# A large weight-gradient store sent as a row scatter, with eight of its 128 rows sent apart

## The chip, the cores and the metric

The kernel runs on one core of one Trainium2 chip. The metric is device time in microseconds (us) of one execution. The six runs of the kernel before lie within 0.2% of each other (730.99 to 732.42 us), so differences of a few tenths of a per cent are read only from several runs on the same chip beside the kernel before.

## The reference

The reference computes one decode step and all its gradients: a layer norm, a 32-head attention over a cache of 8192 positions, and beside it a gated MLP, whose outputs are added.

```python
def _fwd_reference(A_x, A_k_cache, A_v_cache, A_wq, A_wo, B_x, B_w1, B_w3, B_w2):
    # cut: _A_ref is attention with one query row per head; _B_ref is silu(x@w1) * (x@w3) @ w2
    xn = _layernorm(A_x, axis=-1)
    return A_x + _A_ref(xn, A_k_cache, A_v_cache, A_wq, A_wo) + _B_ref(xn, B_w1, B_w3, B_w2)

def reference(...):                      # outputs: out and the gradients of 8 inputs
    _out, _vjp = jax.vjp(_f, A_x, A_k_cache, A_v_cache, A_wq, A_wo, B_w1, B_w3, B_w2)
    ...
```

The caches are (1, 32, 8192, 128) in bf16, so K and V are 67 MB each. They are read once and their gradients are written once. That is 268 MB of the 303.5 MB that the kernel moves. The gradient of w2 is (1728, 640), 2.2 MB.

## The kernel before

One head's K or V is one tile of 128 partitions by 16,384 B (2 MB). It is loaded, used, overwritten by its gradient and stored. Ten such slots rotate. SP (SyncE) issues all these loads and stores in program order.

```python
    def fifo(out_, in_):
        nc.sync.dma_start(out_, in_)
    # cut
    def load_next():
        # cut: next head in turn, next free slot
        fifo(t[:], (kc if kind == "K" else vc)[h])
    # cut
    def store(kind, h):
        t = kv_tiles.pop((kind, h))
        # cut
        fifo((dkc if kind == "K" else dvc)[h], t[:])
        free_slots.append(t)
        load_next()
```

The MLP runs once, early, between the second and the third head. Its weights borrow four of the ten slots. Slot `mD` holds 12 of the 14 row blocks of w2, with 12 rows of 1280 B, or 15,360 B, per partition. Their gradient is written into the same tile and stored from GpSimd. The slot then goes back to the rotation, and SP issues the next load.

```python
    w2a = mD[:, 0:NBA * D].rearrange("p (b c) -> p b c", c=D)
    # cut
        for b in range(NBA):
            nc.vector.tensor_scalar(w2a[:, b, :], g_bc[:], hcol[:, b:b + 1], None, ALU.mult)
        nc.gpsimd.dma_start(out_8[0:NBA * P, :].rearrange("(p fb) c -> p fb c", fb=NBA), w2a)
        # cut: the small rest of w2, from GpSimd too
        free_slots.append(mD)
        load_next()
```

## Time and profile before

| what | before |
|---|---|
| time, median of 3 runs | 732.32 us (731.69 to 732.42) |
| time beside the changed kernel, median of 6 runs | 731.98 us (730.99 to 732.42) |
| span of the profiled run | 729.3 us |
| DMA engines | 90% or more busy in 39 of 40 slices, mean 416 GB/s |
| the stretch 718 to 728 us | no compute; DMA share 0.38, then 0.06 |

The lines themselves stand in the prediction. The page is read for the bound (busy shares, then the digit rows), and the table of windows for the end. There the DMA share is the mean busy share of the 16 engines.

One more view is used below, and this is how to read it. In the trace of the kernel before, the four semaphores that SP alone uses show 1136 steps for 71 transfers, 16 for each. I take them as one step per engine, of which the page counts 16. The time from the first to the last step is called its **lag** here. Read so, it tells how far the slowest of the 16 engines is behind the fastest. I read the steps from the trace's semaphore records; the steps carry no engine names.

### The profile page before, as it was taken

What the parts mean: (1) busy time and instruction counts of PE and PEld (TensorE: products, weight loads), DVE (VectorE), ACT (ScalarE), POOL (GpSimd) and SP (SyncE); (2) the same over time, 40 slices, a digit from 0 to 9 for tenths busy, and PEclk for the clock granted to TensorE, in tenths of its full rate; (3) what the DMA queues carried; (4) which work ended last, traced back from release to release, by engine and by line L of the source; (5) the groups of instructions that cost most, each with busy time, mean ns of one, the idle gap of its engine ahead of it and who ended that gap; (6) DMA issues with size and microseconds to landing.
All of it is one profiled execution on the core that took longest, in us unless ns stands there. A gap on an engine that the chain in (4) does not pass through costs nothing.

```text
span 729.3 us, 12910 instructions
## 1 busy us (share of the span) xinstructions
PE 603.3 (83%) x5193; PEld 376.2 (52%) x5193; DVE 461.1 (63%) x811; ACT 376.1 (52%) x727; POOL 29.9 (4%) x45
## 2 busy tenths in 40 slices
PE   3989589999999999987987987887898879977930
PEld 2546356665566556644554554454465545645510
DVE  4068655677767776767556764655746775667581
ACT  3640736665666656644554554554564545555510
POOL 0010110000100000001000000000000000000000
PEclk9995799999999999999998999998989999999965
DMA  9999999999999999999999999999999999999994
GB/s 344 398 409 422 427 428 425 400 426 422 416 415 428 429 426 424 428 430 426 424 429 429 430 425 427 425 430 429 423 430 425 429 430 429 428 429 429 429 413 183
DMA packets 27135, 303.53 MB, mean 416 GB/s; under 512 B 2798, under 2 KB 4146, under 8 KB 10434
## 3 DMA queue, kind: packets, MB, share of 16 engines
q1 hardware_dynamic: 21328, 276.39, 89.8%
q0 software_dynamic: 5728, 26.30, 8.9%
q8 instruction: 41, 0.67, 0.4%
q14 instruction: 20, 0.16, 0.1%
q10 hardware_dynamic: 18, 0.01, 0.0%
HBM read 151.34 MB, written 151.34 MB: 415 GB/s over the span
## 4 chain that ended last, share of the span: by engine, by line
DMA 48%; PE 38%; DVE 6%; ACT 4%; issue 1%; SPq 0%; ACTq 0%; DVEq 0%
DMA out_dram<-kv 21%; DMA kv<-in_A_k_cache_dram 18%; PE pT L318 18%; DMA kv<-in_A_v_cache_dram 7%; PE sA L339 5%; PE X L433 4%; PE dA L339 4%; DVE kv L466 3%; PE m L356 2%; DMA wo_g<-in_A_wo_dram 2%; ACT KT L320 1%; ACT kv L630 1%; PE gu_ps L549 1%; PE dh_ps L560 1%; PE acc L199 1%
## 5 line engine op out<-in xcount | busy, mean ns | idle before, releaser
L320 ACT COPY KT<-pT 128x512 f32<-128x512 f32 x512 | 288.2, 588 | 228.1 <-PE pT L318 208.6
L318 PE MATMUL pT<-ident_f,kv 128*128 128x128 f32 x2048 | 306.6, 289 | 58.5 <-DMA kv<-in_A_k_cache_dram 32.7
L318 PEld LDWEIGHTS pT<-ident_f,kv 128*128 128x128 f32 x2048 | 235.8, 148 | 151.1 <-PE pT L318 49.7
L466 DVE TENSOR_TENSOR kv<-qd,U 128x4096 bf16<-128x4096 bf16 x64 | 146.0, 2284 | 0.0
L466 DVE TENSOR_TENSOR kv<-qd,P 128x4096 bf16<-128x4096 bf16 x64 | 143.6, 2285 | 0.0
L433 PE MATMUL X<-kv,Z 128*32 128x512 bf16 x1024 | 96.9, 413 | 1.8 <-DVE Z L450 1.8
L339 PE MATMUL dA<-KT,qz 128*32 128x512 bf16 x512 | 83.5, 405 | 0.0
L339 PE MATMUL sA<-KT,qz 128*32 128x512 bf16 x512 | 83.0, 404 | 0.0
L416 DVE SCALAR_TENSOR_TENSOR U<-m,P 128x64 bf16<-128x64 f32 x32 | 7.5, 233 | 85.1 <-PE m L356 85.1
L433 PEld LDWEIGHTS <-Z 128*32 128x32 bf16 x1024 | 33.0, 100 | 35.2 <-issue 8.3
L339 PEld LDWEIGHTS <-qz 128*32 128x32 bf16 x1024 | 29.5, 95 | 40.7 <-issue 38.1
L382 DVE TENSOR_REDUCE mrow<-m 128x1 f32<-128x64 f32 x32 | 7.1, 223 | 68.3 <-PE m L356 68.3
L356 PE MATMUL m<-selc,KT 64*128 64x64 f32 x256 | 30.7, 243 | 8.1 <-ACT KT L346 8.1
L356 PEld LDWEIGHTS m<-selc,KT 64*128 64x128 f32 x256 | 21.7, 145 | 30.2 <-ACT KT L346 20.2
L376 ACT CAST qd<-pT 128x256 bf16<-128x256 f32 x32 | 11.9, 372 | 40.5 <-DVE kv L466 31.5
L389 DVE TENSOR_REDUCE negM<-m 128x1 f32<-128x128 f32 x32 | 9.3, 292 | 33.3 <-PE m L386 33.3
L514 DVE SCALAR_TENSOR_TENSOR wq_g<-wq_g,side 128x512 bf16<-128x512 bf16 x40 | 27.3, 682 | 0.0
L257 DVE SCALAR_TENSOR_TENSOR side<-wo_g,g_bc 128x640 bf16<-128x640 bf16 x32 | 26.2, 820 | 1.0 <-DMA wo_g<-in_A_wo_dram 0.7
L448 DVE SCALAR_TENSOR_TENSOR U<-m,P 128x128 bf16<-128x128 f32 x32 | 11.4, 355 | 16.8 <-PE m L446 16.8
L406 DVE RECIPROCAL rZ<-m 128x1 f32<-128x1 f32 x32 | 5.3, 167 | 24.2 <-PE m L400 24.2
L346 ACT COPY KT<-dA 64x512 f32<-64x512 f32 x32 | 18.6, 582 | 2.7 <-PE dA L339 2.7
L346 ACT COPY KT<-sA 64x512 f32<-64x512 f32 x32 | 18.6, 581 | 1.1 <-PE sA L339 0.8
(161 smaller groups left out, 374.8 us busy)
## 6 DMA issues: line engine op xcount, KB each, us to landing
out_dram<-kv SPq DMA_DIRECT2D x64, 2048.0 KB, 31.0
kv<-in_A_k_cache_dram SPq DMA_DIRECT2D x32, 2048.0 KB, 26.3
kv<-in_A_v_cache_dram SPq DMA_DIRECT2D x32, 2048.0 KB, 26.3
out_dram<-wo_g POOLq DMA_DIRECT2D x8, 640.0 KB, 11.8
out_dram<-wq_g POOLq DMA_DIRECT2D x8, 640.0 KB, 13.2
wq_g<-in_A_wq_dram POOLq DMA_DIRECT2D x7, 640.0 KB, 13.5
wo_g<-in_A_wo_dram POOLq DMA_DIRECT2D x7, 640.0 KB, 19.3
kv<-in_B_w_dram SPq DMA_DIRECT2D x2, 1728.0 KB, 29.3
```

Of the source, the lines that this page charges most:

```text
L257: nc.vector.scalar_tensor_tensor(junk[:], G_["wo"][:, hh, :], 1.0, g_bc[:], ALU.mult, ALU.mult, accum_out=G_["do"][:, hh:hh + 1])
L318: nc.tensor.transpose(pT[:, k * P:(k + 1) * P], W3[:, 4 * c + k, :], ident_f[:])
L320: nc.scalar.copy(KT[:].rearrange("p k w -> p (k w)"), pT[:])
L339: nc.tensor.matmul(S_[kind][q:q + QW, :], lhsT=S_["qz"][:, o:o + QW], rhs=KTb[c][:, par, :], start=(c0 == 0 and par == 0), stop=(c0 == NCH ...
L346: nc.scalar.copy(XS[0:QH].rearrange("p k w -> p (k w)"), S_.pop(kind)[0:QH, :])
L356: nc.tensor.matmul(S_["m"][:, b0:b0 + 4 * J].rearrange("p (x c k t) -> p k x c t", x=4, k=4, t=2)[:, k], lhsT=XS[0:QH, k, :], rhs=selc[0:Q ...
L376: nc.scalar.copy(qd[:].rearrange("p a d -> p (a d)"), hd[h].pop("ps_r"))
L389: nc.vector.tensor_reduce(S_["negM"][:], S_["m"][:, 2 * J:2 * J + P], AX.X, ALU.max, negate=True)
L433: nc.tensor.matmul(xg["X"][q:q + QW, :], lhsT=Z[:, o:o + QW], rhs=W[:, N4 * i:N4 * (i + 1)], start=(slot == 0 and i < 4), stop=(slot == NS ...
L448: nc.vector.scalar_tensor_tensor(S_["U2"][:], S_["V"][:, 0:J].unsqueeze(2).to_broadcast([P, J, 2]), S_["m"][:, OC + NS:OC + NS + 1], S_["P ...
L466: nc.vector.tensor_tensor(dst[:, lo * DH:hi * DH].rearrange("p (j a b) -> p j a b", a=DH // 2, b=2), vec.rearrange("p (a b) -> p a b", b=2 ...
L514: nc.vector.scalar_tensor_tensor(wq_g[:, ci, :], wq_g[:, ci, :], 1.0, dqb, ALU.mult, ALU.mult, accum_out=dxa[:, ci, g:g + 1])
```

## The change

The intent: one engine ends last, so take from it the eight rows of the w2 gradient store that it would carry, and give these rows to engines that end earlier. The store becomes a scatter with a list of row numbers. In the list, the partitions 16-19 and 48-51 get a number past the end (their own plus 256), and such rows are dropped. The dropped rows leave from SP as two transfers of four rows.

```diff
-    masks = consts.tile([P, 4], F32, name="masks")
+    masks = consts.tile([P, 8], F32, name="masks")
@@
+    R0 = 16
+    sidx = masks[:, 4:5].bitcast(mybir.dt.int32)
+    nc.gpsimd.iota(sidx, pattern=[[0, 1]], base=0, channel_multiplier=1)
+    skip = masks[:, 5:6]
+    nc.vector.tensor_reduce(skip, ident_f[:, 0:2 * QW].rearrange("p (a w) -> p a w", w=QW)[:, :, R0:R0 + 4],
+                            AX.XY, ALU.add)
+    nc.vector.scalar_tensor_tensor(sidx, skip, float(2 * P), sidx, ALU.mult, ALU.add)
+
+    def scatter_store(dst, t):
+        nc.gpsimd.indirect_dma_start(out=dst, out_offset=bass.IndirectOffsetOnAxis(ap=sidx, axis=0),
+                                     in_=t, in_offset=None, bounds_check=P - 1, oob_is_err=False)
+        for r0 in (R0, R0 + QW):
+            fifo(dst[r0:r0 + 4], t[r0:r0 + 4])
@@
-        nc.gpsimd.dma_start(out_8[0:NBA * P, :].rearrange("(p fb) c -> p fb c", fb=NBA), w2a)
+        scatter_store(out_8[0:NBA * P, :].rearrange("(p fb) c -> p (fb c)", fb=NBA), mD[:, 0:NBA * D])
```

## The prediction

> **What bounds the kernel now.** I read the page first: busy shares, the slices, the DMA queues, the chain.
>
> ```profile
> span 729.3 us, 12910 instructions
> ...
> PE 603.3 (83%) x5193; PEld 376.2 (52%) x5193; DVE 461.1 (63%) x811; ACT 376.1 (52%) x727; POOL 29.9 (4%) x45
> ...
> DMA  9999999999999999999999999999999999999994
> GB/s 344 398 409 422 427 428 425 400 426 422 416 415 428 429 426 424 428 430 426 424 429 429 430 425 427 425 430 429 423 430 425 429 430 429 428 429 429 429 413 183
> ...
> q1 hardware_dynamic: 21328, 276.39, 89.8%
> q0 software_dynamic: 5728, 26.30, 8.9%
> ```
>
> The 16 DMA engines are at 90% or more in 39 of 40 slices and move 425 to 430 GB/s; no compute engine comes near that (PE 83%). The kernel is bound by transfers: 303.5 MB at 430 GB/s would be 706 us. Only the last slice is poor, at 183 GB/s. So I read the end in a table of windows (columns: stretch, length, then each engine's busy time with its count for PE, PEld, DVE, ACT and POOL, the clock, the DMA share and the GB/s).
>
> ```profile
> 400.00:660.00 260.00, 221.08 (x1874) 136.10 (x1875) 162.24 (x267) 137.15 (x272) 8.17 (x10) 0.94 1.01 428
> 660.00:712.00 52.00, 33.82 (x277) 20.04 (x276) 36.58 (x58) 19.85 (x40) 1.63 (x2) 0.83 0.99 422
> 712.00:718.00 6.00, 0.93 (x3) 0.59 (x3) 1.91 (x11) 0.00 (x0) 0.86 (x1) 0.50 0.84 345
> 718.00:723.00 5.00, 0.00 (x0) 0.00 (x0) 0.00 (x0) 0.00 (x0) 0.00 (x0) 0.50 0.38 157
> 723.00:728.00 5.00, 0.00 (x0) 0.00 (x0) 0.00 (x0) 0.00 (x0) 0.00 (x0) 0.50 0.06 25
> ```
>
> The reader is to see the staircase of DMA shares: 1.01, 0.99, 0.84, 0.38, 0.06. Compute is over by 718, and 0.06 is one sixteenth: in the last 5 us **one DMA engine works alone** at 25 GB/s. The trace's semaphore records say the same. [...] For the last 2 MB store (issued at 705.63) the first step comes at 711.93, the fifteenth 10.8 us later at 722.7 and the sixteenth 16.4 us later at 728.3. One engine ends 5.6 us behind the next. This lag has grown slowly: for the 2 MB transfers the last step trails the first by 3.5 to 4.3 us at 135 to 150 us, by 7 to 8 us around 300, by 10 us around 490, by 14 us at 640. So the end is set by the total work of one engine, which runs with next to no idle, while the others wait for it.
>
> [...] The closing [4, 128] store leaves four packets of 256 B, and following packets back to back (on one engine the next starts 3 to 4 ns before the last ends), these and the other closing small packets lie on engines that end at about 716 to 719, not on the one that ends at 727.9. [...]
>
> **The change part by part.** Removed: one GpSimd store of 1920 KB (128 rows of 15,360 B). Added: a scatter of 120 of these rows from GpSimd, two four-row transfers from SP, and three small setup operations.
>
> *Setup.* An iota on GpSimd and two small DVE operations. Existing DVE reductions of like size cost 0.28 us (128x128 to 128x2) and 0.37 us; the second DVE operation handles one element per partition, some 0.16 us. The vector timeline is idle for 5.73 us before 8.82 us (it waits for g_bc), so the sum of about 0.5 us lies in idle time: 0 us at the end.
>
> *Bytes.* The 15,360 B packets of the present store take 37.3 to 38.4 ns per KB (1000 B), about 0.58 us each. An engine that loses eight of them loses 8 x 0.58 = 4.6 us of work. [...] Total bytes don't change.
>
> *Issue.* These are the issue rows of the timeline around the store, SP's first:
>
> ```profile
> 72.52 0.34 SPq L105 DMA_DIRECT2D kv<-in_A_v_cache_dram  x1
> 77.41 0.34 SPq L105 DMA_DIRECT2D kv<-in_A_k_cache_dram  x1
> 92.03 0.33 SPq L105 DMA_DIRECT2D kv<-in_A_v_cache_dram  x1
> 92.45 0.39 SPq L105 DMA_DIRECT2D kv<-in_A_k_cache_dram  x1
> ```
>
> ```profile
> 77.15 0.56 POOL L612 DMA_DIRECT2D out_dram<-kv  x1 [22.91 <-DVE kv L614]
> 77.69 0.56 POOL L615 DMA_DIRECT2D out_dram<-kv  x1
> 78.25 0.57 POOL L618 DMA_DIRECT2D out_dram<-kv  x1
> ```
>
> The 12 vector operations that fill the tile run from 73.22 to 76.85. The two SP transfers stand between the loads of 72.52 and 77.41, so they issue at about 77 and 77.4 and move the K load by 0.3 us, where transfers queue so deep that the first piece of that load lands at 100.98. [...] The load into the tile's own slot goes out at 92.45; the old store has landed at 91.8, and the load ahead of it waited for another store to 91.9, so a later scatter would delay one load, with two transfers still queued. All this I put at 0 to 0.5 us.
>
> *Sum.* [...] it ends up to 4.6 us earlier, at 723.7, still just behind the others (722.7). But the relief comes at 80 to 90 us and is kept only while that engine always has work. At 126 to 150 us the first engines show lags of 0.0, 0.0 and 0.1 us, so they run dry; the straggler's lag there is at most 3.5 to 4.3 us, and 4.6 us of relief would let it run dry too. I expect 3 to 4.6 us to be left: 732.3 - 3.9 = 728.4.
>
> **Rivals.**
> 1. *Relief of the wrong engine.* [...] the scatter deals rows out differently (in turn, say), so that other engines lose the eight rows. For it: no row names an engine[...]. [...] Time: unchanged, 731.5 to 733.
> 2. *A new wait on SP.* If the four-row transfers are ordered behind the scatter (both write one output tensor), SP stands from 77 to some 92 us instead of to 77.4, and the K load goes out 14 us late. For it: SP takes its work in order. Against: in that stretch the DMA share is 1.00 with a V load, a K store and the w2 stores queued to about 95 us. Time: 0 to +3 us on the above.
> 3. *The scatter is a poor transfer.* Descriptors cut small, or most rows on few engines, would make a new straggler; an extra 8 rows on a slow engine would be +4.6 us. For it: no row for it in this trace. Against: each row is one contiguous run of 15,360 B on both sides. Time: up to 737.
> 4. *The gain is met by another engine.* Several engines end near 722.5, so the gain is capped at 5.6 us whatever the relief.
>
> **Range and chances.** I give 0.6 to relief of the right engine [...], ending near 728.4, 0.3 to no effect near 732, and 0.1 to a loss near 735. The mean is 0.6 x 728.4 + 0.3 x 732 + 0.1 x 735 = 730.1; I choose 729.6, nearer to the likely branch. Range 726.6 to 733.4: the lower end is the full cap of 5.6 us, the upper a loss of 1 us. Two per cent is 14.6 us, over twice the straggler's whole lag behind the next engine, so faster by over 2% gets 0.01, slower 0.02 for a scatter that goes badly, within 2% the other 0.97.
>
> **What would show it.** Right: in the last windows the DMA share no longer has 5 us at 0.06; the last store's sixteenth step follows the fifteenth within 1 to 2 us; bytes and rate in the middle are as before; the two four-row issues lie near 77 us and the next K load within 1 us of 77.4. Wrong: an unchanged 0.06 tail (rival 1); a gap of over 10 us before that K load (rival 2); over 128 packets, or packets far below 15,360 B, for the scatter, or a longer lag of the last step just after 90 us (rival 3). The weakest step is the identity of the straggler, taken from the aim of the change and not from a record; a straggler that differs from run to run would also void it.

The sum came to 732.3 - 3.9 = 728.4 us, the mean over the branches to 730.1, and 729.6 was chosen. The condition of the sum, that the straggler has these rows and that the scatter leaves every row on its engine, was the author's assumption (the "it" that ends earlier is the straggler). Its two chances: 0.8 and 0.75, whose product is the 0.6; 1.2 us for the four-row transfers were set against slack and never entered the sum. A guess of how long the scatter holds GpSimd lay within the 0 to 0.5 us.

## The result

The changed kernel is correct and takes 731.79 us (median of 6 runs, 729.77 to 732.29) against 731.98 us before (6 runs). The ratio is 0.9994, with a 95% interval of 0.9978 to 1.0009: **no difference shown**. A ratio here is the mean time of one kernel's runs over the mean time of the other's runs of the same rounds, so it is not quite the ratio of the medians. A second series of 5 rounds gave 730.55 us (729.3 to 733.18) against 732.23, ratio 0.998 (0.9961 to 0.9998). The two series put the gain at 0.4 and 1.5 us, with intervals from a loss of 0.7 us to a gain of 2.9 us. The 3.9 us of the prediction's favoured branch lie outside both.

From the page of the changed kernel:

```profile
span 730.0 us, 12911 instructions
...
DMA  9999999999999999999999999999999999999993
GB/s 350 397 412 419 422 398 426 408 427 430 427 420 429 428 425 428 425 429 427 426 428 432 425 428 424 429 430 428 424 429 426 430 428 429 431 428 427 428 419 157
...
q1 hardware_dynamic: 21344, 276.51, 89.7%
q0 software_dynamic: 5728, 26.18, 8.9%
```

The bytes have moved as planned: 0.12 MB (8 x 15,360 B) went from q0, GpSimd's queue, to q1. The rate in the middle is as before. The sixth slice (91 to 110 us) fell to 398 GB/s from 428, and the last is no better. The windows of the changed kernel (columns as in the prediction: stretch, length, busy time and count of PE, PEld, DVE, ACT, POOL, clock, DMA share, GB/s):

```profile
92.00:120.00 28.00, 25.53 (x229) 17.19 (x228) 13.33 (x28) 13.87 (x27) 1.30 (x2) 0.94 1.01 407
...
718.00:723.00 5.00, 0.00 (x0) 0.00 (x0) 0.00 (x0) 0.00 (x0) 0.00 (x0) 0.50 0.24 95
723.00:728.00 5.00, 0.00 (x0) 0.00 (x0) 0.00 (x0) 0.00 (x0) 0.00 (x0) 0.50 0.06 26
```

And one window of the kernel before, for the stretch after the w2 store:

```profile
92.00:120.00 28.00, 24.74 (x217) 16.52 (x216) 12.73 (x30) 13.01 (x25) 1.84 (x3) 0.94 1.01 426
```

The reader is to see two things. **The last five microseconds are unchanged**: 0.06, one engine alone. And the stretch just behind the changed store moves 407 GB/s instead of 426. The missing 19 GB/s over 28 us are some 0.53 MB, which is 1.2 us at the full rate. But this is made up later: over the first 250 us the windows give 413 GB/s before and 414 GB/s after. So the dip shows where something goes wrong, and is not by itself a loss at the end.

The issue rows of the changed kernel, GpSimd's first and SP's next (start, duration, engine, line, operation, transfer), and then SP's wait in the stretch 70 to 135 us (total, times, longest):

```profile
75.60 1.24 POOL L191 DMA_INDIRECT out_dram<-kv,masks  x1 [21.52 <-DVE kv L627]
76.81 0.60 POOL L628 DMA_DIRECT2D out_dram<-kv  x1
```

```profile
71.80 0.34 SPq L105 DMA_DIRECT2D kv<-in_A_v_cache_dram  x1
90.87 0.65 SPq L105 DMA_DIRECT2D out_dram<-kv  x2
91.61 0.37 SPq L105 DMA_DIRECT2D kv<-in_A_k_cache_dram  x1
92.07 2.16 SPq L105 DMA_DIRECT2D kv<-in_A_v_cache_dram  x1
103.13 0.33 SPq L105 DMA_DIRECT2D kv<-in_A_k_cache_dram  x1
```

```profile
SPq L105 <- DMA out_dram<-kv,masks: 18.7, 1, 18.7
```

SP stood 18.7 us for the scatter. The two four-row transfers were issued at 90.87, right after the scatter's last landing at 90.81, and the K load behind them at 91.61 instead of 77.41. The load into the slot that the scatter empties went out at 103.13 instead of 92.45. The wait row names the scatter. That the reason is the ordering of two writers of one output tensor is read from the code, not from a record.

The scatter itself came out as hoped. It shows 120 packets of 15,360 B. Its first semaphore step comes at 85.54 and the other fifteen 4.2 to 5.3 us later: one engine had nothing to do. So the dropped rows were not dealt out again, and the eight per engine stayed.

### The profile page after: what moved, and what is told of

It reads as the page before. It is cut to its first block, busy times and chain, and to the rows that moved or that the text cites. A ratio compares the mean times of both kernels' runs of the same rounds, so it can differ in the third digit from the quotient of the medians.

```text
span 730.0 us, 12911 instructions
## 1 busy us (share of the span) xinstructions
PE 597.5 (82%) x5186; PEld 374.2 (51%) x5193; DVE 461.3 (63%) x813; ACT 375.4 (51%) x727; POOL 30.7 (4%) x46
## 4 chain that ended last, share of the span: by engine, by line
DMA 61%; PE 30%; DVE 5%; ACT 2%; issue 1%; SPq 0%; ACTq 0%; DVEq 0%
DMA out_dram<-kv 29%; DMA kv<-in_A_k_cache_dram 19%; PE pT L331 14%; DMA kv<-in_A_v_cache_dram 10%; PE sA L352 4%; PE dA L352 3%; PE X L446 3%; DVE kv L479 2%; PE m L369 2%; DMA wo_g<-in_A_wo_dram 2%; PE gu_ps L562 1%; ACT KT L333 1%; PE dh_ps L573 1%; DVE side L270 0%; PE acc L212 0%
## 5 line engine op out<-in xcount | busy, mean ns | idle before, releaser
L446 PE MATMUL X<-kv,Z 128*32 128x512 bf16 x1024 | 94.3, 405 | 1.8 <-DVE Z L463 1.8
L461 DVE SCALAR_TENSOR_TENSOR U<-m,P 128x128 bf16<-128x128 f32 x32 | 11.4, 355 | 15.7 <-PE m L459 15.7
```

The costliest lines, as they stand in the source:

```text
L446: nc.tensor.matmul(xg["X"][q:q + QW, :], lhsT=Z[:, o:o + QW], rhs=W[:, N4 * i:N4 * (i + 1)], start=(slot == 0 and i < 4), stop=(slot == NS ...
L461: nc.vector.scalar_tensor_tensor(S_["U2"][:], S_["V"][:, 0:J].unsqueeze(2).to_broadcast([P, J, 2]), S_["m"][:, OC + NS:OC + NS + 1], S_["P ...
```

## The experiments

Twelve kernels ran. Three questions were open. Is the straggler the engine that the change aims at? Does the relief reach the end? And if it does not, does SP's wait, the slow rows, or the early hour lose it? Kernels are compared only within the same rounds. Several give a wrong result, and this is said with each.

| run | median us (range) | before, same chip | ratio (95%) |
|---|---|---|---|
| e1_late4 | 728.43 (727.18-728.92) | 732.42 | 0.9944 (0.993-0.9957) |
| e1_late9 | 733.4 (732.34-733.95) | 732.42 | 1.0014 (1.0001-1.0028) |
| e2_skip_only | 729.68 (729.05-731.2) | 732.42 | 0.9963 (0.9949-0.9976) |
| e0_after | 730.55 (729.3-733.18) | 732.23 | 0.998 (0.9961-0.9998) |
| e5_act | 732.15 (730.91-733.79) | 732.23 | 0.9996 (0.998-1.0012) |
| e8_scatter_all | 731.4 (730.84-731.62) | 732.23 | 0.9987 (0.9973-1.0001) |
| e6_late | 730.48 (729.84-731.55) | 732.23 | 0.998 (0.9965-0.9994) |
| e9_mid4 | 726.26 (725.81-727.73) | 731.91 | 0.9929 (0.9915-0.9943) |
| e10_ports | 730.02 (727.19-731.2) | 731.91 | 0.997 (0.9953-0.9987) |
| e11_lateV | 730.13 (728.75-730.55) | 731.91 | 0.9973 (0.9959-0.9986) |
| e12_mid_ok | 728.4 (726.12-729.99) | 731.82 | 0.9951 (0.9936-0.9965) |

### Which engine is the straggler: e1_late4 and its control e1_late9

The kernel before, with only its last K store (head 31, at about 705 us) sent as a scatter that drops the eight rows. Nobody writes them. The author took the scatter to count rows from the start of the tensor, which no run here tests, so the rows are sent to head 0's place. Both kernels are wrong. The control drops the partitions 68-71 and 100-103, so it has the same bytes and the same scatter, but other rows.

```diff
-        fifo((dkc if kind == "K" else dvc)[h], t[:])
+        if kind == "K" and h == H - 1:
+            scatter_store(dkc[0], t[:])        # e1_late4: drops 16-19, 48-51; e1_late9: 68-71, 100-103
+        else:
+            fifo((dkc if kind == "K" else dvc)[h], t[:])
```

> The kernel before, with the last store alone (K gradient of the last head, 128 rows of 16,384 B) as a row scatter that leaves out partitions 16-19 and 48-51, unwritten, so one engine has 8 packets of 0.61 us less, too late to lose the relief by idling. Wrong result on purpose (that store goes to the first head's place, eight rows are missing). Theory A (those rows are the straggler's, the change lost its gain before the end): the end comes 4.9 us earlier, ratio 0.9933, and the tail with a DMA share of 0.06 is gone. Theory B (the straggler is another engine): the end and the tail stay, ratio 1.000.

> Control for the late scatter: the same, but the rows left out are partitions 68-71 and 100-103[...]. Theory A: no gain, ratio 1.000, tail as before. If it gains 4.9 us too, it is the scatter itself or the missing bytes and not the engine; if it alone gains, that engine is the straggler.

Measured: 0.9944, that is 4.1 us less than before, and 1.0014, 1.0 us more. The windows of e1_late4 and then of the control:

```profile
718.00:723.00 5.00, 0.00 (x0) 0.00 (x0) 0.00 (x0) 0.00 (x0) 0.00 (x0) 0.50 0.13 53
723.00:728.00 5.00, 0.00 (x0) 0.00 (x0) 0.00 (x0) 0.00 (x0) 0.00 (x0) 0.56 0.01 2
```

```profile
723.00:728.00 5.00, 0.00 (x0) 0.00 (x0) 0.00 (x0) 0.00 (x0) 0.00 (x0) 0.50 0.06 25
```

The 0.06 tail goes when exactly the rows 16-19 and 48-51 are dropped, and it stays when eight others are. This settles that **the straggler is the engine of these rows** in this scatter. The scatter alone gains nothing (the control is 1.0 us slower). So the aim of the change is right, and what failed lies between 90 us and the end.

### A marker that failed: e4_markers

The kernel before with 48 tiny loads at the end, to read off each engine's finish. Which loads were to put a packet between those of the straggler rested on an assumption that no run here shows.

```diff
+    for rep in range(3):
+        for n in range(1, 17):
+            w = 10 + n
+            nc.scalar.dma_start(mark[0:n, at:at + w], A_wo[0:n, 0:w])
+            at += w
```

> The kernel before with 48 tiny loads from the ACT queue after its last store, of 1 to 16 rows in three turns, each row count with its own size. Its time is of no matter. [...] a marker of n rows puts a packet between the straggler's 16 KB packets[...].

It ran correctly and took 747.11 us in one look (state unknown). The waits of SP in 640 to 746 us show why it tells nothing:

```profile
SPq L105 <- DMA KT<-in_A_wo_dram: 18.4, 2, 11.2
```

SP's last stores waited for the landing of the marker loads, so the end that was to be measured was pushed aside by the measuring. All 16 engines ended the last store within 0.2 us of each other, near 736.7. The run is inconclusive.

### The scatter without the eight rows: e2_skip_only

The changed kernel without the two four-row transfers. It is wrong, since the eight rows are never written.

```diff
-        for r0 in (R0, R0 + QW):
-            fifo(dst[r0:r0 + 4], t[r0:r0 + 4])
```

> The changed kernel without its two four-row transfers (eight rows of the w2 gradient stay unwritten, wrong on purpose), so SP has nothing to wait for at 77 us. Theory A with the loss put down to SP's wait: the K load issues at 77 again and 3 to 4.6 us show at the end, ratio 0.994 to 0.996. Theory A with the loss put down to idling at 120 to 150 us whatever SP does: the load issues at 77 and the end stays within 1.5 us. Theory B (wrong engine relieved): the end stays, ratio 1.000.

Measured: 0.9963, or 2.7 us less (interval 1.8 to 3.7), which lies between the first two branches. SP's issues and the window after the store:

```profile
77.14 0.34 SPq L105 DMA_DIRECT2D kv<-in_A_k_cache_dram  x1
91.61 0.33 SPq L105 DMA_DIRECT2D kv<-in_A_v_cache_dram  x1
92.03 0.42 SPq L105 DMA_DIRECT2D kv<-in_A_k_cache_dram  x1
```

```profile
92.00:120.00 28.00, 25.52 (x216) 17.12 (x215) 11.80 (x28) 13.00 (x25) 1.30 (x2) 0.88 1.01 425
...
723.00:728.00 5.00, 0.00 (x0) 0.00 (x0) 0.00 (x0) 0.00 (x0) 0.00 (x0) 0.50 0.06 25
```

SP's wait and the late slot load are gone (77.14 and 92.03, as before), and the rate behind the store is back at 425. Yet even with nothing sent in place of the rows the tail of one engine is there, and the relief of 8 x 0.58 = 4.6 us shows up as 2.7. The steps show when it goes. Lags after the store, in us:

| transfer landing near | after | e2_skip_only |
|---|---|---|
| 85 to 98 us, second step behind the first | 4.0 at 91 | 3.1 at 91, 4.3 at 97 |
| 120 us, second step behind the first | 0.3 at 116 | 2.6 at 120 |
| 135 us, next three steps behind the first | 0.1, 0.3, 0.3 | 0.1, 0.2, 0.2 |
| 695 us, last step (before: 15.7) | 16.2 | 15.0 |

At 85 to 98 us one engine is 3 to 4 us ahead of the other fifteen. At 135 us several engines complete within 0.3 us of each other: nobody is ahead any more. The reading that fits e2_skip_only is that the leading engine finds its queue empty and waits for the next transfer, while the others catch up. The packet records support it: from 120 to 135 us the 16 engines together spend 3.2 to 4.6 us more without a packet than in any of the five kernels that have relieved nobody by then (before, e1_late4, e1_late9, e8_scatter_all, e9_mid4). That it is the relieved engine that leads is argued from the rows, since the steps carry no names.

The changed kernel itself seems to lose its lead in another way, because its packets leave no more idle time from 92 to 150 us than those of the kernel before. Its trace shows this instead. From 92.50 to 99.48 us one engine carries 13 packets of GpSimd's stores one after another. It is the leading one: its share of those two stores lands at 97.55 and 99.81, 8.8 and 10.4 us before any other engine's. The 13 packets of 6,912 B take 0.44 to 0.58 us each, where the median of such packets is 0.262 us, so 3.4 us more in all. No run tests that this is what used up the relief, or why the packets are slow.

### Does SP's wait cost it: e5_act and e8_scatter_all

In e5_act the four-row transfers are issued from ACT, after its copies for the MLP, so SP never stands. The result is correct.

```diff
-        for r0 in (R0, R0 + QW):
-            fifo(dst[r0:r0 + 4], t[r0:r0 + 4])
+    def four_rows(dst, t):                     # called after the MLP's broadcast copies
+        for r0 in (R0, R0 + QW):
+            nc.scalar.dma_start(dst[r0:r0 + 4], t[r0:r0 + 4])
```

> The changed kernel, correct, but the two four-row transfers issue from ACT after its bc casts, where ACT has nothing to do until about 100 us, so SP no longer stands behind the scatter. Theory W (SP's wait until the scatter lands, and the late load into the freed slot, eat the gain): the K load issues near 77 again, the next but one near 93 in place of 103, and the ratio is 0.996 to 0.997 as without the four rows. Rival theory X (the missing 123 KB[...] made the run without the four rows faster): the ratio stays at 0.999 to 1.000.

Measured: 0.9996, no gain. SP's issues in e5_act:

```profile
76.62 0.34 SPq L105 DMA_DIRECT2D kv<-in_A_k_cache_dram  x1
91.69 0.33 SPq L105 DMA_DIRECT2D kv<-in_A_v_cache_dram  x1
102.76 0.33 SPq L105 DMA_DIRECT2D kv<-in_A_k_cache_dram  x1
```

The K load goes out at 76.62 again, but the load into the emptied slot still goes at 102.76: it has to wait for the eight rows, which ACT issued at 92.29. The stretch of 120 to 150 us then moves 398 GB/s, where the kernel before moves 408. So **SP's wait alone is not the loss**, but the late load into the slot remains.

In e8_scatter_all the scatter keeps all 128 rows (the factor on the skip mask is 0) and there are no four-row transfers. The result is correct. It is the change of the store's form alone.

```diff
-    nc.vector.scalar_tensor_tensor(sidx, skip, float(2 * P), sidx, ALU.mult, ALU.add)
+    nc.vector.scalar_tensor_tensor(sidx, skip, 0.0, sidx, ALU.mult, ALU.add)
@@
-        for r0 in (R0, R0 + QW):
-            fifo(dst[r0:r0 + 4], t[r0:r0 + 4])
```

> The changed kernel with all 128 rows in the scatter and no four-row transfers; correct. If the relief of one engine is what counts: 1.000, no engine lands early at the scatter (first to sixteenth step within 1.5 us), the tail with a DMA share of 0.06 stays. If the scatter itself, or its issue from GpSimd, is what gains or loses: off 1.000 by over 0.2%.

Measured: 0.9987 with an interval that reaches 1, so the form itself costs nothing that these runs show. Its steps follow each other within 1.7 us from 90.71 on, with no leader, so the leader in the changed kernel comes from the dropped rows.

The changed kernel itself ran as e0_after. Its result stands above (0.998).

> The changed kernel once more, on one chip with the three below, for a tighter interval: 0.9994 was measured, so 0.998 to 1.001.

### Are the eight rows slow: e10_ports

The four-row packets of the changed kernel take 1.5 to 4.1 us each, but for one at 0.573 us; the scatter's packets of the same size take 0.573 us (one 0.747). Each transfer takes four neighbouring partitions. Does that make its packets slow? In e10_ports the two transfers carry the partitions 0, 4, 8, 12 and 32, 36, 40, 44 instead, four apart. It is wrong, since the dropped rows are never written.

```diff
-        for r0 in (R0, R0 + QW):
-            fifo(dst[r0:r0 + 4], t[r0:r0 + 4])
+        for r0 in (0, QW):
+            fifo(dst[r0:r0 + 16:4], t[r0:r0 + 16:4])
```

> The changed kernel, but its two four-row transfers carry partitions 0, 4, 8, 12 and 32, 36, 40, 44 (written twice with the same data; the eight rows stay unwritten, wrong on purpose): same count, size and issue[...]. Theory P (the four-row packets take 1.5 to 4.5 us in place of 0.57[...]): now 0.57 to 0.7 us each, landing within 4 us of the issue, and the load into the freed slot goes out near 95 in place of 103; the ratio goes from 0.998-0.9995 toward 0.9963. Rival Q (four-row transfers are slow as such): packets and load as late as before.

Measured: the packets take 0.573 to 0.586 us (one 1.133). **The slow rows are slow because of where they lie**, and not as four-row transfers as such. The edit moves the rows in the output too, so the run does not tell the place in the tile from the place in the output, and why the place counts was not shown. In the run e6_late below, the last four packets of such rows, 16,384 B each, took 2.45 to 2.54 us, that is 26.7 GB/s for the four (65,536 B in 2.45 us). (The four before them, with other transfers still under way, took 4.1 to 4.2 us.) The time is 0.997, 2.2 us less than before, and the rate in 92 to 120 us is 419 GB/s. The intervals do not part it from the changed kernel. But two parts of the expectation are missed. The rows landed 6.3 and 7.1 us after their issue, not within 4, and the slot's load went out at 101.09 us, not near 95. The fast packets started only at 97.6, though SP had issued them at 93.17 and 93.97. A V load was still queued ahead of them on SP, which would explain it. So the fast packets shorten the rows, not the wait ahead of them.

### Is it the early hour: e9_mid4

The kernel before, with the same drop in the K store of the 17th head, issued at 399.42 us. It is wrong, like e1_late4.

```diff
+        if kind == "K" and h == H // 2:
+            scatter_store(dkc[0], t[:])        # drops 16-19, 48-51
+        else:
+            fifo((dkc if kind == "K" else dvc)[h], t[:])
```

> The same omission of partitions 16-19 and 48-51 (8 packets less for one engine, wrong on purpose), now in the K store of the seventeenth head, at about 390 us. Theory M (only the stage up to 150 us, where engines run dry, wastes relief; later the straggler never idles): as much as at the end, 4 us, ratio 0.994 to 0.995. Theory N (relief before the last stores is used up wherever it is given, because the other engines wait for the same buffers): within 1.5 us, ratio 0.998 to 1.000.

Measured: 0.9929, or 5.2 us less, and the end has changed:

```profile
718.00:723.00 5.00, 0.00 (x0) 0.00 (x0) 0.00 (x0) 0.00 (x0) 0.00 (x0) 0.50 0.28 120
723.00:728.00 5.00, 0.00 (x0) 0.00 (x0) 0.00 (x0) 0.00 (x0) 0.00 (x0) 0.68 0.00 0
```

The tail is gone entirely, and the lag near 695 us is 10.4 instead of 15.7. The size fits as well: here the packets are 16,384 B and take 0.61 us, so eight are 4.9 us, inside the measured interval of 4.2 to 6.2. (That 0.13 MB are moved by nobody brings nothing by itself: the control e1_late9 leaves out as much.) The same drop at 76 us without replacement (e2_skip_only) gained 2.7 us and left the tail. So **relief given at mid-run is kept whole, and relief given at 80 to 90 us only in part**, even where nothing is sent in place of the rows.

### Versions that are correct: e6_late, e11_lateV and e12_mid_ok

If late relief pays, it needs, on the assumption named at e1_late4, a store whose place is at the start of its tensor. In e6_late the heads are worked in reverse order, so that head 0's K gradient is the last store, sent as the scatter, and the eight rows follow from SP. In e11_lateV it is the last V store, and the last K store is plain and goes ahead of the eight rows. In e12_mid_ok the heads are rotated by 16, so that head 0's K gradient leaves at 399 us, and the eight rows follow behind the next V store. In all three the w2 store is as before. The core of e12_mid_ok (cut: the same rotation of the weights' groups):

```diff
-        fifo(t[:], (kc if kind == "K" else vc)[h])
+        fifo(t[:], (kc if kind == "K" else vc)[(h + H // 2) % H])
@@
-        fifo((dkc if kind == "K" else dvc)[h], t[:])
+        dst = (dkc if kind == "K" else dvc)[(h + H // 2) % H]
+        if kind == "K" and h == H // 2:
+            scatter_store(dst, t[:])           # e6_late: h == H - 1, heads reversed; e11_lateV: the last V
+        else:
+            fifo(dst, t[:])
+            if late:
+                late.pop()()                   # the two four-row transfers
```

> A correct version of the late relief: the w2 store as before, heads worked on in the opposite order (so that the last head's gradient starts its tensor[...]), the last K store as a scatter without partitions 16-19 and 48-51, and these as two four-row transfers from SP, which has nothing else left then. If late relief is kept whole: 4 us earlier, ratio 0.994 to 0.995, as with the rows left out. If the four rows, issued only once the scatter has landed (about 717), end the kernel themselves: 724 to 727, ratio 0.995 to 0.999.

> Correct, for a version that beats both: heads in the opposite order, relief in the last V store (scatter at about 701), the plain K store next, and the two four-row transfers after it on SP, once the scatter has landed at about 712. If their slow packets end by 721: the end near 724, ratio 0.994 to 0.995. If they end last again, as with the K store (727): 0.997 to 0.999.

> A correct version of the relief at mid-run: heads in an order turned by sixteen, so that the first head's K gradient is stored at about 390 us; that store is the scatter without partitions 16-19 and 48-51, and the two four-row transfers issue on SP behind the next V store, when the scatter has landed, some 20 us before the slot is loaded again. If the relief is kept and the slow four-row packets lie in the slack[...]: the tail with a DMA share of 0.06 is gone, the end 4 to 5.6 us earlier, ratio 0.992 to 0.995. If the four rows[...] take from the relieved engine what it gained: ratio 0.997 to 1.000.

Measured: e6_late 0.998 and e11_lateV 0.9973, 1.5 and 2.0 us less. In both the eight rows are now what ends last. In e6_late the scatter has landed at 718.84 and the slow rows end at 727.16; in e11_lateV they end at 727.75. The straggler is relieved and its rows, in packets of 2.45 to 4.2 us in e6_late, take its place.

e12_mid_ok gives 0.9951, 3.6 us less, and **beats both kernels** (the changed kernel's ratios are 0.9994 and 0.998). SP's issue of a V store and the two four-row transfers, the GB/s row of its page, and its last window:

```profile
428.58 1.22 SPq L105 DMA_DIRECT2D out_dram<-kv  x3
```

```profile
GB/s 353 400 410 421 428 427 424 410 423 423 421 421 427 431 425 423 426 431 426 423 429 429 428 425 404 425 430 427 423 430 426 431 427 431 429 427 426 431 429 230
```

```profile
723.00:728.00 5.00, 0.00 (x0) 0.00 (x0) 0.00 (x0) 0.00 (x0) 0.00 (x0) 0.50 0.02 10
```

The tail is down to a third, and the last store's sixteenth step is 3.5 us behind the fifteenth, where it was 5.6. The ratio lies between the two branches of the expectation. But the 25th slice (436 to 454 us) shows 404 GB/s where the kernel before has 427: it is the hour of the eight slow rows, whose first packets start at 448.58 and take 3.2 to 3.6 us. The lag near 685 us is 13.0, so of the 5.3 us that e9_mid4 keeps about half is kept here. That the dip at the slow rows eats the rest fits both numbers. It was not tested by itself. Nor was the changed order of the heads: no run has the new order without the relief, so these three ratios hold for both together.

## Why the prediction was right or wrong

The time lies inside the stated range, but by luck and not by the text's main step, since the range also took in no effect at all. The favoured branch did not come: the text put 3.9 us of gain in its main step, and the result is nearest to its branch of no effect, for which it gave another reason (the wrong engine). Point by point:

- **The bound and the tail: right.** Bytes and the rate in the middle are as they were, and one engine ends alone. (One reading was too generous: the 39 busy slices move 344 to 430 GB/s and not 425 to 430. The sums do not rest on it.)
- **The condition of the sum: right as far as it was tested.** That the straggler is the engine of the eight rows was called the weakest step, and was an assumption. e1_late4 (4.1 us less) against its control (1.0 us more) shows it, and the one early step of the changed kernel's scatter (85.54, the others from 89.74 on) shows that the eight rows are one engine's in it. That the plain store has them on one engine too was not shown. Its number stays unknown, as no record gives numbers. Rivals 1 and 3 fall. Rival 4, the cap by the next engine, shows in e9_mid4, where the last store's sixteenth step follows the fifteenth by 0.4 us.
- **Size of the relief, 4.6 us: right.** 4.1 us late in the run and 5.2 at mid-run, where packets are a little larger.
- **Setup, 0 us: right.** The two added DVE operations take 0.15 and 0.16 us and the iota 0.13, and DVE's idle time before that point is still 4.94 us. The scatter held GpSimd for 1.24 us, against 0.56 us for the plain store.
- **Issue near 77 us: wrong, and rival 2 came true to the letter**: 90.87 for the rows, 91.61 for the K load. Its price was within what rival 2 allowed, since e5_act, without this wait, is no faster.
- **"All this I put at 0 to 0.5 us" for the slot's load: mis-sized.** The load went out 10.7 us late (103.13 for 92.45), and the stretch behind it moved 0.53 MB less, which was made up by 250 us. The text weighed only a later scatter, not the wait for the eight rows.
- **The four-row transfers, 1.2 us: mis-sized.** The text counted two more packets of 0.58 us for each engine that takes them. The packets took up to 4.1 us instead of 0.573. Why was not shown; e10_ports only ties it to the place of the rows.
- **"I expect 3 to 4.6 us to be left": this is the step that failed.** Between nothing and 1.5 us were left. Two of its terms were too small. The first is the early hour. The text named the condition, that relief is kept only while that engine always has work, and saw engines run dry at 126 to 150 us (the first lags of 0.0, 0.0 and 0.1 us, so read), but allowed 1.6 us for it. Without any rows in place, e2_skip_only kept 2.7 of 4.6 us, so 1.9 were lost, while the same drop at 399 us lost nothing (e9_mid4). The text's own figures pointed there: a straggler that is 3.5 to 4.3 us behind and gets 4.6 us of relief is no longer behind, and what it then waits is lost. The second is what the replacement costs, the two points above: e2_skip_only gains 2.7 us and the changed kernel 0.4 (0.9994) to 1.5 (0.998), so another 1.2 to 2.3 us. The two need not simply add up: in the changed kernel's own trace the loss that can be seen lies at 92 to 99 us, and no extra idle time is left for 120 us.

Some of this stays open. Taking SP's wait away gives nothing measurable (e5_act), and fast rows give 2.2 us against the kernel before (e10_ports), nearly what no rows give. That would put most of the replacement's cost on the slow packets, but each interval is 0.3 to 0.4% wide, so these parts of one or two microseconds are not told apart. No run takes away both the wait and the slow packets while the rows are still sent. The steps and the times also disagree by some microseconds: by the steps the lead of e2_skip_only is wholly gone at 135 us, and its tail in the one profile is hardly shorter (lag 15.0 for 15.7), yet it runs 2.7 us faster over its runs. Its profiled run was at the slow end of them, 730.85 us for a median of 729.68, so the profile may show less than the runs kept; no run settles it.

## What to carry to other kernels

When transfers bind, look at the last windows: a DMA share of one sixteenth (0.06 here) was read as one engine that ends alone, and the steps of the semaphores tell since when it falls behind (here the lag of the last step grows from some 4 us at 150 us to 15.7 at 695). Work taken from it at 399 us gained 5.2 us, at 76 us only 2.7. The reading is that it counts only if the engine has work queued from then to the end, so take it after the last stretch in which engines run dry, and try it first by simply dropping the rows late and dropping other rows as a control. Look also at what is put in its place: here the replacement's packets took up to 4.1 us instead of 0.573, and SP stood 18.7 us for it. How much each of the two costs at the end was not shown.
